# Thirteen waits of GpSimd on VectorE in a fused linear-attention and PReLU feed-forward kernel

## The chip, the cores and the metric

The kernel runs on one core of a Trainium2 chip. The metric is the device time of one execution in microseconds; the median over the runs stands for a kernel. The profile is one further execution, taken by the hardware profiler, whose own time is given beside its span (first to last instruction).

## The reference

Decayed linear attention over blocks, and then a feed-forward layer with a PReLU between its two products (all in float32, cut to what is computed):

```python
# q, k, v: (4, 8, 768, 64); lam: one decay per head; block = 64
for b in range(nb):
    intra = (q_b @ k_b^T * Dmask) @ v_b            # Dmask[i, j] = lam**(i-j) for i >= j, else 0
    inter = (q_b * lam**(pos+1)) @ kv_state
    out_b = intra + inter
    kv_state = lam**block * kv_state + (k_b * lam**(block-1-pos))^T @ v_b
x = out as (3072 tokens, 512)
h = x @ w_in                                       # 512 x 2048
g = maximum(h, 0) + alpha * minimum(h, 0)
y = g @ w_out                                      # 2048 x 512
```

## The kernel before

The tokens are worked through in six groups `c` of 512 (256 positions of two batches). Each group has four attention units, numbered 4c to 4c+3 (a batch and four of the eight heads), so there are 24 units, of which each works on two blocks of 128 positions. The attended output of a group is written, transposed and in float16, to `XT[c]`, and is the moving operand of the first product of the feed-forward layer.

For unit n the steps are: `cast` (queries or keys to float16), `turn` and `turn_copy` (TensorE transpose into PSUM, and its copy to `qkT`; later units use a DMA transpose, `turned`), `decayed` (L336: queries times decay, to `qdT`), `key_decayed` (L281: keys times decay, to `kdec`), `score_products` and `masked` (L385: scores times the decay mask, to `sm`), then on TensorE `inter` (queries with the state `R`), `intra` (`sm` with the values), `state_products` (keys with values), and after these `attended` (L431: PSUM to `XT`), `first_state` (L447: the new state after the first block, on ScalarE) and `states` (L453: the decayed state plus the new product, on VectorE). `inter`, `intra` and `state_products` of all units share one PSUM tile, `acc`, so that `inter` of the next unit stands behind `attended`, `first_state` and `states` of the one before.

The feed-forward layer takes group 0 in the plain way: `up` (16 blocks of 128 hidden features), `relu` on ScalarE and `prelu` (L513) on VectorE, `down` into `o_ps`. From group 1 on the second product, and for groups 4 and 5 the first one too, is made by a scheme of seven products in place of eight (Strassen-Winograd), which needs sums and differences of operand quarters: `w_sum(i, k)` (L558) for `w_out`, `in_sum(i, k)` (L694) for `w_in`, `g_sum` (L580) for the hidden activations, `x_sum` for the inputs. `i` says which sum, `k` which quarter of it. Each of these calls is one subtraction or addition of two float16 operands of 128x512 in SBUF (lines L550 and L553), on VectorE, or on GpSimd where the last argument is `"G"`. The product in seven parts begins at the call `second(1, 1, 0)`, long behind the place of the change.

The program is written out by hand as one list of calls (L776 to L1818). The order of the calls is the order of each engine's own instructions; between engines the framework puts semaphore waits where data or buffers demand them. Nothing else keeps, say, GpSimd behind VectorE. GpSimd also issues DMAs (`load_v16`, `load(..., "G")`, `load_win`, `load_wout`), in the same order as its other instructions; the other loads, the stores and the DMA transposes stand in the queue of SyncE.

The calls that the change touches stand in the list as follows: `w_sum(1, 0)` at L1023 (t1 on VectorE, between `decayed(7, "V")` and `attended(5, "V")`), `key_decayed(6)` at L996 (GpSimd), `in_sum(1, 0)` at L1061, `cast(9, "q16", "G")` at L1040, `decayed(8)` at L1072 and `w_sum(2, 0)` at L1077.

Of the kernel before, what the change touches and what calls it, by code (L numbers as in the profile page):

```python
# [11 lines left out]
def kernel(  # L12
# [229 lines left out]
    XT = {}  # L242
    units = [(c, bi, hh) for c in range(NC) for bi in range(2) for hh in range(2)]

    def copy_on(eng, out, in_):
        if eng == "A":
            nc.scalar.activation(out, in_, AF.Copy)  # L247
        elif eng == "V":
            nc.vector.tensor_copy(out=out, in_=in_)
        else:  # L250
            nc.gpsimd.tensor_copy(out=out, in_=in_)
# [178 lines left out]

    def attended(n, eng):  # L431
        co, bo, ho = units[n]
        if co not in XT:
            pool, tag = (raw_pool, "kraw") if co == 5 else (xt_pool, "xT")
            XT[co] = pool.tile([128, NHP, 2, 2, L], fp16, tag=tag, name="xT")
        copy_on(
            eng,
            XT[co][:, ds(2 * ho, 2), :, bo, :].rearrange("p h e (a j) -> p a (h e) j", a=2),
            acc[:, :, 0:256].rearrange("p a (he j) -> p a he j", j=64),
        )  # L440

# [66 lines left out]
    def relu(c, f, bi=None):  # L508
        n = CH if bi is None else W
        m = M[c, f, bi] = m_pool.tile([128, CH], fp32, tag="m", name="m")  # L510
        nc.scalar.activation(m[:, 0:n], HP[c, f, bi][:, 0:n], AF.Relu, scale=-1.0)  # L511

    def prelu(c, f, bi=None):  # L513
        g, m, h = g_of(c, f), M[c, f, bi], HP[c, f, bi]
        if bi is None:
            g = g.rearrange("p e b j -> p (e b j)")
        else:
            g = g[:, :, bi, :]
            m, h = (y[:, 0:W].rearrange("p (e j) -> p e j", e=2) for y in (m, h))
        nc.vector.scalar_tensor_tensor(  # L520
            out=g, in0=m, scalar=oma[:, f : f + 1], in1=h, op0=ALU.mult, op1=ALU.add
        )
# [23 lines left out]
    T_OUT = {}  # L546
    HALF = DM // 2

    def sub(out, a, b, eng="V"):
# [251 lines left out]
    query_decay(1, 1)  # L801
    cast(0, "q16", "V")
    turn(1, (1,))
    turn_copy(1, (1,), "V")
# [23 lines left out]
    cast(2, "k16", "A")  # L828
    cast(3, "q16", "G")
    turn(2, (0,))  # L830
    turn_copy(2, (0,), "V")
# [59 lines left out]
    up(0, 6)  # L891
    prelu(0, 4, 0)
    relu(0, 5)
# [39 lines left out]
    prelu(0, 1)  # L933
    prelu(0, 4, 1)
    relu(0, 0)
# [59 lines left out]
    turn_copy(6, (0,), "V")  # L995
    key_decayed(6)  # L996
    masked(5)
# [5 lines left out]
    key_decayed(7, "V")  # L1003
    decayed(6, "V")
    turn_copy(7, (1,), "A")
    down(0, 3, 2)
# [12 lines left out]
    load(2, 0, "k", 1)  # L1019
    decayed(7, "V")  # L1020
    down(0, 2, 3)
    down_copy(0, 3)
    w_sum(1, 0)  # L1023
    attended(5, "V")
# [14 lines left out]
    first_state(6)  # L1039
    cast(9, "q16", "G")  # L1040
    down_store(0, 2)
# [13 lines left out]
    state_products(8)  # L1055
    w_sum(3, 0)
    query_decay(3, 0)
    w_sum(4, 3)
    load(3, 1, "k", 1)
    prelu(1, 3, 0)  # L1060
    in_sum(1, 0)  # L1061
    score_products(8)
# [8 lines left out]
    up(1, 0)  # L1071
    decayed(8)  # L1072
    states(6, (1,))
    w_sum(3, 3)
    key_decayed(11)
    key_decayed(9)
    w_sum(2, 0)  # L1077
    masked(8)
# [21 lines left out]
    up(1, 15)  # L1100
    w_sum(3, 1)
    up(1, 5)
    relu(1, 7)
# [35 lines left out]
    decayed(9)  # L1139
    prelu(1, 3, 1)  # L1140
    w_sum(3, 2, "G")
    relu(1, 9)
    load_v16(14)
# [50 lines left out]
    second(1, 6, 0)  # L1194
    g_sum(1, 4, 0, 0)
    masked(10)
    g_sum(1, 4, 1, 1, "G")
# [3 lines left out]
    inter(10)  # L1201
    g_sum(1, 4, 1, 0, "G")
    key_decayed(17, "A")
    intra(10)
# [260 lines left out]
    second(2, 5, 1)  # L1465
    decayed(22, "V")
    cast(23, "k16", "G")
    prelu(3, 9)
# [17 lines left out]
    prelu(3, 7)  # L1486
    g_sum(3, 1, 0, 1, "G")
    relu(3, 14)
    second_store(1, 7)
# [359 lines left out]
```

## Time and profile before

| what | value |
|---|---|
| median of 3 runs | 203.97 us (203.88 to 205.3) |
| the profiled execution's own time | 205.24 us |
| its span, first to last instruction | 203.5 us |
| mean granted TensorE clock | 0.989 |
| busy: TensorE, VectorE, GpSimd, ScalarE | 195.1, 175.3, 143.6, 130.9 us |

A row of the timeline gives start in the span, duration, engine, line of the program, operation, output<-input, shape and, in brackets, how long the engine had been idle before it and what released it. Rows that follow one another with the same name are merged, with their count. The records of neighbouring instructions of one engine overlap by some 0.05 to 0.1 us. Buffer numbers are left out in names, so that `t<-w_out_sb` is `w_sum(1, k)` and `t<-w_out_sb,t` is `w_sum(2, k)` or `w_sum(4, k)`.

### The profile page before, as it was taken

The page shows a single profiled execution, that of the slowest core. Times are in us where ns is not written, and L with a number is a line of the kernel's source. Part 1 is how long each engine was busy: PE and PEld are TensorE (multiplying, and loading weights), DVE is VectorE, ACT ScalarE, POOL GpSimd, SP SyncE. Part 2 cuts the span into 40 slices and gives each one's busy share as a digit, 9 for nine tenths or more (in the row PEclk, how much of TensorE's full clock was granted, in tenths as well). Part 3 has the DMA queues.
Part 4 walks back from the last instruction along what each step waited for, and adds up shares of the span by engine and source line. Part 5 has one row for each costly group of instructions (what it writes and reads, how often), then busy time and mean ns, then how long its engine had stood idle before and what let it go on. Part 6 is the DMA issues. An engine that isn't in the chain of part 4 may idle for free.

```text
span 203.5 us, 5865 instructions
## 1 busy us (share of the span) xinstructions
PE 195.1 (96%) x2351; PEld 129.9 (64%) x2351; DVE 175.3 (86%) x320; ACT 130.9 (64%) x281; POOL 143.6 (71%) x161
## 2 busy tenths in 40 slices
PE   7999999995999999999999999999999999999992
PEld 7775454544544498766565768766665656788892
DVE  6988789998989999899999998889989999995800
ACT  5895774426587699687777769455596987533022
POOL 8999859794495948999999979970386222656700
PEclk9999999998899999999999999999999999999999
DMA  5999999999949998999999953230040001103143
GB/s 163 280 196 228 242 269 231 199 291 224 229 52 180 278 239 236 205 223 168 196 293 169 132 77 80 78 106 0 0 156 3 0 2 52 55 19 138 45 152 116
DMA packets 59199, 30.53 MB, mean 150 GB/s; under 512 B 29652, under 2 KB 57956, under 8 KB 59172
## 3 DMA queue, kind: packets, MB, share of 16 engines
q1 hardware_dynamic: 41236, 19.87, 40.1%
q0 software_dynamic: 17776, 10.23, 35.7%
q8 instruction: 18, 0.29, 0.6%
q14 instruction: 9, 0.07, 0.1%
q10 hardware_dynamic: 160, 0.07, 0.1%
HBM read 27.27 MB, written 6.29 MB: 165 GB/s over the span
## 4 chain that ended last, share of the span: by engine, by line
PE 80%; DVE 6%; DMA 4%; POOL 4%; issue 2%; ACT 1%; DVEq 0%; POOLq 0%; ACTq 0%
PE h_ps L498 26%; PE y L632 16%; PE b L632 12%; PE b L757 5%; DMA w_in_sb<-in_moe_w_in_dram 4%; PE o_ps L528 4%; PE e L757 3%; PE a L757 3%; PE acc L402 3%; PE s L377 3%; PE acc L361 2%; POOL v L272 2%; PE acc L422 1%; DVE sm L388 1%; PE tp L316 1%
## 5 line engine op out<-in xcount | busy, mean ns | idle before, releaser
L498 PE MATMUL h_ps<-xT,w_in_sb 128*128 128x512 f16 (+1 forms) x264 | 59.6, 373 | 0.2 <-DMA w_in_sb<-in_moe_w_in_dram 0.2
L632 PEld LDWEIGHTS <-g 128*128 128x128 f16 x464 | 44.7, 98 | 10.1 <-DVE g L550 0.6
L520 DVE SCALAR_TENSOR_TENSOR g<-m,oma,h_ps 128x512 f16<-128x512 f32 (+1 forms) x66 | 46.0, 727 | 3.9 <-ACT m L511 2.8
L511 ACT ACTIVATE m<-h_ps 128x512 f32<-128x512 f32 (+1 forms) x66 | 37.4, 582 | 15.8 <-PE h_ps L498 14.8
L498 PEld LDWEIGHTS <-w_in_sb 128*128 128x128 f16 x264 | 24.4, 98 | 25.5 <-DMA w_in_sb<-in_moe_w_in_dram 1.1
L388 DVE TENSOR_TENSOR sm<-s,dmask 128x1024 f16<-128x1024 f32 x24 | 29.3, 1219 | 2.2 <-PE s L377 2.2
L632 PE MATMUL y<-w_out_sb,g 128*128 128x256 f16 x224 | 27.9, 273 | 0.3 <-DVE g L550 0.3
L550 POOL TENSOR_TENSOR g<-g 128x512 f16<-128x512 f16 x11 | 13.2, 1204 | 16.4 <-DVE s L553 16.3
L341 POOL TENSOR_TENSOR qdT<-qkT,qdecay 128x512 f16<-128x512 f16 (+1 forms) x20 | 21.0, 1056 | 4.7 <-ACT qkT L247 2.6
L632 PE MATMUL b<-t,g 128*128 128x256 f16 x160 | 19.8, 273 | 0.0
L247 ACT ACTIVATE xT<-acc 128x512 f16<-128x512 f32 x22 | 13.1, 595 | 9.6 <-PE acc L422 5.6
L272 POOL DMA_DIRECT2D v<-in_v_dram x24 | 18.8, 789 | 0.0
L457 DVE SCALAR_TENSOR_TENSOR R<-R,rdecay,acc 128x128 f16<-128x128 f16 x54 | 15.6, 342 | 2.8 <-ACT xT L247 2.2
L550 POOL TENSOR_TENSOR g<-g,g 128x512 f16<-128x512 f16 x12 | 14.3, 1204 | 5.0 <-DVE g L550 2.9
L553 POOL TENSOR_TENSOR s<-g,g 128x512 f16<-128x512 f16 x9 | 10.4, 1155 | 8.4 <-DVE g L520 8.4
L528 PE MATMUL o_ps<-w_out_sb,g 128*128 128x512 f16 x64 | 16.1, 395 | 0.0
L247 ACT ACTIVATE o_sb<-y 128x512 f32<-128x512 f32 (+2 forms) x12 | 6.2, 526 | 13.1 <-PE y L674 7.1
L290 ACT ACTIVATE kdec<-kraw,kdecay 128x64 f16<-128x64 f32 x56 | 14.0, 343 | 0.0
L292 POOL TENSOR_TENSOR kdec<-kraw,kdecay 128x512 f16<-128x512 f32 x13 | 13.8, 1068 | 0.0
L361 PE MATMUL acc<-qdT,R 128*128 128x128 f16 x80 | 8.4, 219 | 2.2 <-DVE R L457 2.0
L377 PE MATMUL s<-qkT 64*64 64x128 f16 x384 | 10.3, 222 | 0.2
L402 PE MATMUL acc<-sm,v 64*64 64x128 f16 x384 | 10.1, 224 | 0.1
(130 smaller groups left out, 371.0 us busy)
## 6 DMA issues: line engine op xcount, KB each, us to landing
out_dram<-o_sb SPq DMA_DIRECT2D x23, 256.0 KB, 2.5
kraw<-in_k_dram SPq DMA_DIRECT2D x7, 512.0 KB, 5.8
qraw<-in_q_dram SPq DMA_DIRECT2D x6, 512.0 KB, 5.6
v<-in_v_dram POOLq DMA_DIRECT2D x24, 128.0 KB, 5.2
w_in_sb<-in_moe_w_in_dram POOLq DMA_DIRECT2D x4, 512.0 KB, 7.9
w_out_sb<-in_moe_w_out_dram POOLq DMA_DIRECT2D x4, 512.0 KB, 9.6
qraw<-in_q_dram POOLq DMA_DIRECT2D x6, 256.0 KB, 7.1
qraw<-in_q_dram SPq DMA_DIRECT2D x6, 256.0 KB, 5.6
```

Source lines behind the costliest of these rows:

```text
L247: nc.scalar.activation(out, in_, AF.Copy)
L272: nc.gpsimd.dma_start(out=v16.rearrange("p h e d -> p h (e d)"), in_=v[2 * (c % 2) + bi, ds(4 * hh, 4), ds((c // 2) * W, W), :].rearrange( ...
L341: engine(eng).tensor_tensor(out=qdT[:, :, :, p], in0=(t["qps"] if eng == "P" else t["qkT"][:, 0])[:, :, :, p], in1=qdecay[:, hh, :, :, p], ...
L377: nc.tensor.matmul(t["s"][ds(a * 64, 64), hl, hp, 1 - e, :].rearrange("p (e j) -> p e j", e=2), lhsT=t["qkT"][p, 1, e, hp, ds(a * 64, 64)] ...
L388: nc.vector.tensor_tensor(out=t["sm"].rearrange("p a h x j -> p (a h) x j"), in0=t["s"].rearrange("p a h x j -> p (a h) x j"), in1=mask_of ...
L498: nc.tensor.matmul(h[:, 0:n] if bi is None else h[:, 0:n].rearrange("p (e j) -> p e j", e=2), lhsT=w_in_sb[:, gi, ts(f, 128)], rhs=x.rearr ...
L511: nc.scalar.activation(m[:, 0:n], HP[c, f, bi][:, 0:n], AF.Relu, scale=-1.0)
L520: nc.vector.scalar_tensor_tensor(out=g, in0=m, scalar=oma[:, f : f + 1], in1=h, op0=ALU.mult, op1=ALU.add)
L528: nc.tensor.matmul(O[c, t], lhsT=g_of(c, f)[:, t // 2, t % 2, :], rhs=w_out_sb[:, f, :], start=(f == 0), stop=(f == NF - 1),)
L550: engine(eng).tensor_tensor(out=out, in0=a, in1=b, op=ALU.subtract)
L632: nc.tensor.matmul(Y[c, k][:, ds(b * HALF, HALF)], lhsT=left(c, i, f, b), rhs=right(i, f), start=(f == 0 and b == 0 and i in (1, 5)), stop ...
L757: nc.tensor.matmul(t, lhsT=w, rhs=x, start=(g == 0 and i in (1, 5)), stop=(g == 1), skip_group_check=True)
```

## The change

A new helper, `vector_turn(n)`, remembers the VectorE instruction that was issued last, and `gpsimd_waits(m)` makes the GpSimd instruction that was issued last wait for the remembered one of number m. There are thirteen calls of the second. They fall on eight GpSimd instructions, since some wait for two or three. Some calls change their place in the list, so that the remembered instruction stands ahead of the one that waits. `attended` and `prelu` are rewritten with options that no call uses; what they issue is the same.

```diff
+    TURN = {}
+    def newest(engine_type):
+        return next(i for i in reversed(tc.nc.cur_bb.bb.instructions) if i.engine == engine_type)
+    def vector_turn(n):
+        TURN[n] = newest(mybir.EngineType.DVE)
+    def gpsimd_waits(n):
+        tc.add_manual_dep(
+            newest(mybir.EngineType.Pool),
+            TURN[n].name,
+            mybir.DependencyInfo(mybir.DependencyClass.Sync, mybir.DependencyReason.DATA),
+            reason="VectorE goes first",
+        )
...
     cast(0, "q16", "V")
+    vector_turn(0)
...
     cast(3, "q16", "G")
+    gpsimd_waits(0)
...
     turn_copy(6, (0,), "V")
-    key_decayed(6)
+    w_sum(1, 0)
+    vector_turn(1)
     masked(5)
...
     key_decayed(7, "V")
     decayed(6, "V")
+    vector_turn(2)
+    decayed(7, "V")
+    vector_turn(3)
+    key_decayed(6)
+    gpsimd_waits(2)
+    gpsimd_waits(1)
+    gpsimd_waits(3)
...
-    decayed(7, "V")
     down(0, 2, 3)
     down_copy(0, 3)
-    w_sum(1, 0)
     attended(5, "V")
...
-    cast(9, "q16", "G")
+    in_sum(1, 0)
+    vector_turn(4)
...
     w_sum(3, 0)
+    vector_turn(5)
+    w_sum(4, 3)
+    vector_turn(6)
+    cast(9, "q16", "G")
+    gpsimd_waits(6)
+    gpsimd_waits(4)
+    gpsimd_waits(5)
     query_decay(3, 0)
-    w_sum(4, 3)
     load(3, 1, "k", 1)
-    prelu(1, 3, 0)
-    in_sum(1, 0)
+    prelu_half(1, 3, 0)
...
-    decayed(8)
     states(6, (1,))
     w_sum(3, 3)
+    vector_turn(7)
+    w_sum(2, 0)
+    vector_turn(8)
+    decayed(8)
+    gpsimd_waits(8)
     key_decayed(11)
+    gpsimd_waits(7)
+    gpsimd_waits(8)
     key_decayed(9)
-    w_sum(2, 0)
...
     w_sum(3, 1)
+    vector_turn(9)
...
     w_sum(3, 2, "G")
+    gpsimd_waits(9)
...
     g_sum(1, 4, 0, 0)
+    vector_turn(10)
...
     g_sum(1, 4, 1, 0, "G")
+    gpsimd_waits(10)
...
     decayed(22, "V")
+    vector_turn(11)
...
     g_sum(3, 1, 0, 1, "G")
+    gpsimd_waits(11)
```

What it does to the engines' instructions is seen in three places. The order is unchanged on TensorE, ScalarE, GpSimd and SyncE; on VectorE two instructions move, and on GpSimd seven get a wait for VectorE that they had not, or a later one.

The first place is on VectorE, where the scores of unit 5 are masked. `sm` is written by `masked(5)`, `t1` by `w_sum(1, 0)`, `t2` and `t4` by `w_sum(2, 1)` and `w_sum(4, 1)`, `kdec` by `key_decayed(7)`, `qdT` by `decayed(6)` and `decayed(7)`, `xT` by `attended(5)`. Before:

```order
L249 COPY qkT_983<-tp_978 128x512 [waits PE_49,Pool_49]
L388 TENSOR_TENSOR sm_987<-s_905,dmask_175 128x1024 [waits DVE_49]
L550 TENSOR_TENSOR t2_963<-w_out_sb_122,t1_818 128x512 [waits DMASW7_49]
L550 TENSOR_TENSOR t4_1001<-w_out_sb_122,t2_963 128x512 [waits DVE_49]
L292 TENSOR_TENSOR kdec_1003<-kraw_709,kdecay_176 128x512 [waits DMASW3_49]
L341 TENSOR_TENSOR qdT_1005<-qkT_983,qdecay_181 128x4x64
L341 TENSOR_TENSOR qdT_1086<-qkT_961,qdecay_181 128x4x64
L550 TENSOR_TENSOR t1_818<-w_out_sb_122 128x512 [waits DMASW1_49]
L249 CAST xT_973<-acc_126 128x2x4x64 [waits PE_49,Activation_49]
```

and with the change (the lines of the same helpers have other numbers there):

```order
L249 COPY qkT_983<-tp_978 128x512 [waits PE_49,Pool_49]
L573 TENSOR_TENSOR t1_818<-w_out_sb_122 128x512 [waits DMASW1_49]
L388 TENSOR_TENSOR sm_986<-s_905,dmask_175 128x1024 [waits DVE_49]
L573 TENSOR_TENSOR t2_963<-w_out_sb_122,t1_818 128x512 [waits DMASW7_49]
L573 TENSOR_TENSOR t4_1000<-w_out_sb_122,t2_963 128x512 [waits DVE_49]
L292 TENSOR_TENSOR kdec_1002<-kraw_709,kdecay_176 128x512 [waits DMASW3_49]
L341 TENSOR_TENSOR qdT_1004<-qkT_983,qdecay_181 128x4x64
L341 TENSOR_TENSOR qdT_1006<-qkT_961,qdecay_181 128x4x64
L249 CAST xT_973<-acc_126 128x2x4x64 [waits PE_49,Activation_49]
```

`w_sum(1, 0)` moved from just ahead of `attended(5)` to just ahead of `masked(5)`; the others kept their order.

The second place is on GpSimd, from `load_v16(8)` (the first row) over `cast(6, "k16")`, `key_decayed(6)`, `key_decayed(8)`, `cast(10, "k16")`, `cast(9, "q16")`, `load_v16(9)` and `cast(10, "q16")` to `decayed(8)`. The difference with its waits:

```order
 L272 DMA v_969<-in_v_dram 128x4x128
 L251 CAST qk_922<-kraw 128x512 [waits DMAHW5_49]
-L292 TENSOR_TENSOR kdec<-kraw,kdecay 128x512
+L292 TENSOR_TENSOR kdec<-kraw,kdecay 128x512 [waits DVE_49]
 L292 TENSOR_TENSOR kdec<-kraw,kdecay 128x512 [waits DMAHW6_49]
 L251 CAST qk_1111<-kraw 128x512 [waits DMAHW0_49,PE_49,Pool_49]
-L251 CAST qk_1152<-qraw 128x512 [waits DMAHW7_49,PE_49,Pool_49]
+L251 CAST qk_1245<-qraw 128x512 [waits DMAHW7_49,DVE_49,PE_49]
 L272 DMA v_1278<-in_v_dram 128x4x128 [waits DMASW4_49]
 L251 CAST qk_1111<-qraw 128x512 [waits DMAHW2_49]
-L341 TENSOR_TENSOR qdT<-qkT,qdecay 128x512 [waits Activation_49]
+L341 TENSOR_TENSOR qdT<-qkT,qdecay 128x512 [waits DVE_49,Activation_49]
```

Three instructions gained a wait for VectorE: `key_decayed(6)` for `decayed(7)`, `cast(9, "q16")` for `w_sum(4, 3)`, `decayed(8)` for `w_sum(2, 0)` (of several remembered instructions the last one counts).

The third place is on VectorE behind `masked(7)`, where `qkT` is written by `turn_copy(6)`, `t1` by `w_sum(1, 2)`, `qk16` by `cast(8, "q16", "V")` and `sm` by `masked(6)`. Before, and then with the change:

```order
L388 TENSOR_TENSOR sm_1108<-s_1062,dmask_175 128x1024 [waits PE_49]
L249 COPY qkT_983<-tp_1101 128x512 [waits PE_49]
L550 TENSOR_TENSOR t1_818<-w_out_sb_122 128x512
L249 CAST qk16_1149<-qraw_1021 128x512 [waits DMAHW7_49]
L388 TENSOR_TENSOR sm_1202<-s_1167,dmask_175 128x1024 [waits PE_49]
```

```order
L388 TENSOR_TENSOR sm_1108<-s_1065,dmask_175 128x1024 [waits PE_49]
L249 COPY qkT_983<-tp_1101 128x512 [waits PE_49]
L576 TENSOR_TENSOR s1_775<-w_in_sb_121 128x512
L573 TENSOR_TENSOR t1_818<-w_out_sb_122 128x512
L249 CAST qk16_1149<-qraw_1024 128x512 [waits DMAHW7_49]
L388 TENSOR_TENSOR sm_1201<-s_1166,dmask_175 128x1024 [waits PE_49]
```

`in_sum(1, 0)`, which writes `s1`, came in ahead of `w_sum(1, 2)`; before, it stood behind `prelu(1, 3, 0)`.

More of the change, by code (lines that the diff above doesn't have):

```diff
@@ L429, in state_products, with attended @@
                         )
-    def attended(n, eng):
+    def attended(n, *how):
         co, bo, ho = units[n]
@@ L435, in attended @@
             XT[co] = pool.tile([128, NHP, 2, 2, L], fp16, tag=tag, name="xT")
[L436 to L440, printed above, removed]
+        x = XT[co][:, ds(2 * ho, 2), :, bo, :].rearrange("p h e (a j) -> p a (h e) j", a=2)
+        o = acc[:, :, 0:256].rearrange("p a (he j) -> p a he j", j=64)
+        if len(how) == 2:
+            x, o = x[:, how[0]], o[:, how[0]]
+        copy_on(how[-1], x, o)
     KV = {}
@@ L511, in relu, with prelu, prelu_half, prelu_of @@
         nc.scalar.activation(m[:, 0:n], HP[c, f, bi][:, 0:n], AF.Relu, scale=-1.0)
-    def prelu(c, f, bi=None):
+    def prelu(c, f, eng="V"):
+        prelu_of(c, f, None, eng)
+    def prelu_half(c, f, bi):
+        prelu_of(c, f, bi, "V")
+    def prelu_of(c, f, bi, eng):
         g, m, h = g_of(c, f), M[c, f, bi], HP[c, f, bi]
@@ L519, in prelu @@
             m, h = (y[:, 0:W].rearrange("p (e j) -> p e j", e=2) for y in (m, h))
-        nc.vector.scalar_tensor_tensor(
+        engine(eng).scalar_tensor_tensor(
             out=g, in0=m, scalar=oma[:, f : f + 1], in1=h, op0=ALU.mult, op1=ALU.add
@@ L891 @@
     up(0, 6)
-    prelu(0, 4, 0)
+    prelu_half(0, 4, 0)
     relu(0, 5)
@@ L933 @@
     prelu(0, 1)
-    prelu(0, 4, 1)
+    prelu_half(0, 4, 1)
     relu(0, 0)
@@ L1139 @@
     decayed(9)
-    prelu(1, 3, 1)
+    prelu_half(1, 3, 1)
     w_sum(3, 2, "G")
+    gpsimd_waits(9)
     relu(1, 9)
```

## Prediction

> **What bounds the kernel now.** I read the page first, then the waits and the windows around the one deep hole in TensorE, then the timelines of VectorE, GpSimd and TensorE there.
>
> ```profile
> span 203.5 us, 5865 instructions
> PE 195.1 (96%) x2351; PEld 129.9 (64%) x2351; DVE 175.3 (86%) x320; ACT 130.9 (64%) x281; POOL 143.6 (71%) x161
> PE   7999999995999999999999999999999999999992
> ```
>
> TensorE is busy for 195.1 of 203.5 us. The row of slices shows a ramp at the start, the drain at the end, and one hole in between, the 5 of slice ten. An edit that doesn't touch the hole has little to win. The waits from 43 to 50 us name it:
>
> ```profile
> ACT R L449 <- DVE xT L249: 3.1, 1, 3.1
> PE acc L361 <- DVE R L457: 2.0, 1, 2.0
> ```
>
> TensorE waits 2.0 us, once, for the state update of unit 7 (`states(7)`, L457), which follows `first_state(7)` on ScalarE (L449), which waits for `attended(5)` on VectorE (L249). The windows show a second cost (columns: stretch, its length, busy PE, PEld, DVE, ACT and POOL, granted clock):
>
> ```profile
> 45.56:48.98 3.42, 1.40 (x18) 0.92 (x18) 2.97 (x5) 1.83 (x4) 1.87 (x4) 1.00 1.20 254
> 48.98:52.39 3.41, 3.38 (x57) 2.01 (x56) 2.92 (x7) 1.30 (x4) 1.29 (x2) 0.50 0.89 196
> 52.39:55.80 3.41, 3.41 (x69) 2.14 (x68) 3.41 (x8) 2.62 (x7) 1.61 (x2) 1.00 0.95 245
> ```
>
> In the stretch with the hole TensorE was busy for 1.40 of 3.42 us (41%); in the next stretch of that length the granted clock was 0.50, and then 1.00 again. So the hole seems to be paid twice. VectorE tells where it comes from:
>
> ```profile
> 39.24 1.22 DVE L388 TENSOR_TENSOR sm<-s,dmask 128x1024 f16<-128x1024 f32 x1
> 40.37 0.87 DVE L550 TENSOR_TENSOR t<-w_out_sb,t 128x512 f16<-128x512 f16 x2
> 41.16 0.68 DVE L292 TENSOR_TENSOR kdec<-kraw,kdecay 128x512 f16<-128x512 f32 x1
> 41.77 1.71 DVE L341 TENSOR_TENSOR qdT<-qkT,qdecay 128x256 f16<-128x256 f16 x2
> 43.40 3.11 DVE L550 TENSOR_TENSOR t<-w_out_sb 128x512 f16<-128x512 f16 x1
> 46.44 0.68 DVE L249 CAST xT<-acc 128x512 f16<-128x512 f32 x1
> 47.56 0.61 DVE L457 SCALAR_TENSOR_TENSOR R<-R,rdecay,acc 128x128 f16<-128x128 f16 x2 [0.45 <-ACT R L449]
> 48.08 1.22 DVE L388 TENSOR_TENSOR sm<-s,dmask 128x1024 f16<-128x1024 f32 x1
> 49.55 0.42 DVE L550 TENSOR_TENSOR t<-w_out_sb 128x512 f16<-128x512 f16 x1
> ```
>
> The same subtraction takes 0.42 us at 49.55 (`w_sum(1, 2)`) and 3.11 us at 43.40 (`w_sum(1, 0)`, just ahead of `attended(5)`). GpSimd, meanwhile:
>
> ```profile
> 38.35 1.17 POOL L553 TENSOR_TENSOR s<-w_in_sb 128x512 f16<-128x512 f16 x1
> 41.18 1.69 POOL L550 TENSOR_TENSOR t<-w_out_sb,t 128x512 f16<-128x512 f16 x1 [1.66 <-DMA w_out_sb<-in_moe_w_out_dram]
> 42.81 0.79 POOL L272 DMA_DIRECT2D v<-in_v_dram  x1
> 43.59 0.62 POOL L251 CAST qk<-kraw 128x512 f16<-128x512 f32 x1
> 44.17 2.05 POOL L292 TENSOR_TENSOR kdec<-kraw,kdecay 128x512 f16<-128x512 f32 x2
> 47.77 0.61 POOL L251 CAST qk<-kraw 128x512 f16<-128x512 f32 x1 [1.55 <-DMA kraw<-in_k_dram]
> 48.32 0.61 POOL L251 CAST qk<-qraw 128x512 f16<-128x512 f32 x1
> ```
>
> The slow subtraction ends at 46.51, 0.29 us after `key_decayed(6)` and `key_decayed(8)` (44.17 to 46.22). I take it that VectorE with two operands in SBUF and GpSimd exclude one another, and that the one that waits ends some 0.3 us after the other is done. `decayed(6)` and `decayed(7)` (1.71 us together) lose time in the same way to `w_sum(2, 3, "G")` at 41.18.
>
> The Trainium skill ("SBUF — State Buffer", section "Who interferes with whom") says that such a pair shares a port as a lock, held for a whole instruction by whichever issues first, while the other blocks fully. The first half agrees with the 0.29 us. The second does not: `w_sum(1, 0)` began at 43.40, ahead of the cast at 43.59, and was passed by three instructions. By the rule alone it would have ended by 43.40 + 0.42 = 43.82, and something other than GpSimd would have held it: that is rival C.
>
> **The change part by part.** *1. `w_sum(1, 0)` moves ahead of `masked(5)`* to 39.24, where `in_sum(1, 3, "G")` runs to 39.52, so that it ends by 39.52 + 0.29 = 39.81. `masked(5)` then runs from 39.73 to 40.95 and `w_sum(2, 1)` to about 41.3. Bounds of this part's stall: 0 and 0.15. Next, `w_sum(2, 3, "G")`, which a DMA releases at 41.18, now comes ahead of `w_sum(4, 1)`. It needs 1.17 us (as its like at 38.35) and is done at about 42.45, `w_sum(4, 1)` at 42.75, `key_decayed(7)` at 43.35. TensorE takes that one's `kdec` in the L422 of this view:
>
> ```profile
> 43.38 0.42 PE L402 MATMUL acc<-sm,v 64*64 64x128 f16 x16
> 43.62 0.29 PE L422 MATMUL acc<-v,kdec 64*64 64x64 f16 x16
> 43.75 0.40 PE L377 MATMUL s<-qkT 64*64 64x128 f16 x16
> 44.08 1.90 PE L528 MATMUL o_ps<-w_out_sb,g 128*128 128x512 f16 x8
> 45.81 0.39 PE L316 MATMUL tp<-ident,qk 128*128 128x128 f16 x4
> 48.22 0.27 PE L361 MATMUL acc<-qdT,R 128*128 128x128 f16 x2 [2.02 <-DVE R L457]
> 49.36 0.64 PE L402 MATMUL acc<-sm,v 64*64 64x128 f16 x16
> 52.36 0.63 PE L316 MATMUL tp<-ident,qk 128*128 128x128 f16 x8
> ```
>
> There, at 43.62, 0.27 us are left. `decayed(6)` and `decayed(7)` need about 0.4 each (at 41.77 the first was held until 42.87 + 0.29 = 43.16, and the pair ended at 43.48); between them stands `cast(6, "k16")` of GpSimd, which costs them 0.6 + 0.3 at most. They end between 44.0 and 44.5.
>
> *2. `key_decayed(6)` waits for `decayed(7)`.* Without that, it and `key_decayed(8)` could pass `decayed(7)` as they passed `w_sum(1, 0)`. It starts at 44.5 in place of 44.17. Behind it on GpSimd stand `key_decayed(8)` (then done at 46.6) and `cast(10, "k16")`, which a DMA releases only at 47.77, so nothing is pushed on.
>
> *3. `attended(5)`* so starts at 44.4 in place of 46.44, 2.0 us earlier, and with it `first_state(7)`, `states(7)` (47.56) and `masked(7)` (48.08). `inter(7)` becomes ready at 46.2, just as TensorE ends its transposes (45.81 + 0.39). **The hole of 2.02 us goes.** Bounds: 1.0 (if two more blockings of 0.5 fall into the chain) and 2.1 (`masked(7)` still sets `intra(7)`, and can't come more than 0.1 earlier than the rest allows).
>
> *4. The half clock* goes with the hole. From `intra(7)` at 49.36 to the transposes at 52.36 lie 3.0 us. At full clock the same pieces, by the starts of the rows from 43.38 on, take 0.24 (L402), 0.33 (L377), 0.86 (four of the eight L528, 45.81 − 44.08 = 1.73 for eight) and some 0.25 for small products: 1.7 us. So 1.3 us are won; bounds 0 and 1.4.
>
> *5. The third place costs a little.* `in_sum(1, 0)` (0.42) now stands ahead of `w_sum(1, 2)` and of `cast(8, "q16", "V")`, which feeds the transposes at 52.36. With `cast(10, "k16")` at 47.77 crossing, that cast ends at about 49.15 and TensorE is ready at 49.05: 0.15 lost; bounds 0 and 0.5.
>
> *6. `cast(9, "q16")` waits for `w_sum(4, 3)`, `decayed(8)` for `w_sum(2, 0)`.* The rows are:
>
> ```profile
> 51.93 0.42 DVE L550 TENSOR_TENSOR w_out_sb<-w_out_sb 128x512 f16<-128x512 f16 x1
> 52.26 0.42 DVE L550 TENSOR_TENSOR t<-w_out_sb,t 128x512 f16<-128x512 f16 x1
> 54.23 1.40 DVE L550 TENSOR_TENSOR t<-w_out_sb,t 128x512 f16<-128x512 f16 x1
> ```
>
> ```profile
> 54.19 1.16 POOL L341 TENSOR_TENSOR qdT<-qkT,qdecay 128x512 f16<-128x512 f16 x1 [2.58 <-ACT qkT L247]
> ```
>
> `w_sum(4, 3)` ended at 52.68. Now it comes behind `cast(8, "q16", "V")` (49.15), `masked(6)` (1.2, as at 48.08) and `w_sum(3, 0)` (0.34), so at 51.0. The cast goes from 48.32 to there, and what is queued behind it on GpSimd goes with it: the `v` DMA (0.79), `cast(10, "q16")` (0.61) and `decayed(8)` (1.16), which ends at about 51.0 + 0.6 + 0.8 + 0.6 + 1.2 = 54.2 in place of 55.35 − 3.2 = 52.15. TensorE asks for it in `inter(8)`, at 59.78 (row below) − 3.2 = 56.6: 2.4 us of cover. If that were gone, each microsecond of lateness would cost one. The stall of `w_sum(2, 0)` (1.40 for 0.42) goes, under the same cover.
>
> ```profile
> 59.78 0.39 PE L361 MATMUL acc<-qdT,R 128*128 128x128 f16 x4
> ```
>
> *7. The other new waits* are met already: `w_sum(3, 2, "G")` starts at 64.63, its VectorE partner ends at 61.71, and the three others too start behind their partner's end, so that they cost nothing; the cover is GpSimd's own work ahead of them, and without it each would cost GpSimd, not TensorE, the wait for one short instruction.
>
> ```profile
> 61.28 0.43 DVE L550 TENSOR_TENSOR w_out_sb<-w_out_sb 128x512 f16<-128x512 f16 x1
> ```
>
> ```profile
> 64.63 1.16 POOL L550 TENSOR_TENSOR w_out_sb<-w_out_sb 128x512 f16<-128x512 f16 x1
> ```
>
> **Sum:** 2.0 + 1.3 − 0.15 = 3.2 (3.15), and behind 56 us TensorE runs without a hole, so the shift should reach the end. The profiled execution took 205.24 us, 1.74 more than its span: 205.24 − 3.2 = **202.0**. The median of 203.97 is 1.27 us lower than that execution, the size of term 4; I read it as executions in which the hole is split so that no half clock follows. They lose terms 3 and 5 alone: 203.97 − 1.85 = 202.1, which agrees.
>
> **The rivals.** *A: the half clock is in the median's executions too,* and the 1.27 us are the profiler's. Then 203.97 − 3.2 = 200.8. For it speaks that profiling may cost time; against it, that one plain run took 205.3.
>
> *B: the clock drop has nothing to do with the hole* and stays. Then only terms 3 and 5 come off the profiled execution: 205.24 − 1.85 = 203.4. The 41% ahead of it speak against this. The Trainium skill ("TensorE: Matmul & The Clock Gate", section "What's actually happening") lets the clock fall after an idle window of about 3.4 us; by that, a gap of 2.02 us would not suffice, and the result would be this rival's. The trace agrees with the window's length, not with the need for a wholly idle one.
>
> *C: the stall travels with the instruction.* If `w_sum(1, 0)` waits for something else than GpSimd, it takes 3.11 us at 39.24 too. The sum of VectorE's work ahead of `attended(5)` is the same, which again starts at 46.44: no change, 204.0. Against it: the end 0.29 us after GpSimd's.
>
> *D, slower: `w_sum(4, 1)` is passed as `w_sum(1, 0)` was.* It stands between `w_sum(2, 3, "G")`, the `v` DMA and `cast(6, "k16")`, which end at 42.45, 43.24 and 43.86. Then `w_sum(4, 1)` ends at 44.15, `key_decayed(7)` at 44.8, and TensorE waits at 43.62 for `kdec`, 1.2 us; `inter(7)` comes at 47.4 in place of 48.22, and if the half clock follows this hole too, 205.24 − 0.8 = 204.4, 0.2% above the median. It decides once `key_decayed(7)` ends after 43.62. For it: that order of three has been passed once. Against: `decayed(6)`, in a like place, was not.
>
> **How the numbers follow.** My forecast 0.60, A 0.13, B 0.07, C 0.12, D 0.08. A measurement of this kernel can tell about 1% from no change, that is 201.93 or less as faster, over 206.0 as slower. Half of the forecast lies under 201.93, since its terms spread by 0.4 us: 0.30, with A 0.43 for faster. Slower by over 1% needs D with more than its price: 0.04. The rest, 0.53, is within 1%. The range 200.7 to 203.8 leaves out a part of A (0.05), most of C (0.10) and a half of D (0.04).
>
> **What would show it.** Right: `w_sum(1, 0)` in some 0.5 us near 39.3; `attended(5)` near 44.4; no idle of TensorE over 0.5 us from 43 to 50; a granted clock of 1.00 from 48.98 on; `decayed(8)` ending 2 us ahead of `inter(8)`. Wrong: a gap of TensorE at its L422 near 43.6 (D), a subtraction of 3 us at 39 (C), a half clock without a hole (B), or new idle of TensorE behind 56 us that gives the shift back.

## The result, and the profile after

| | before | changed |
|---|---|---|
| median, 6 executions each, by turns on the same chip | 204.78 us (203.88 to 205.54) | 201.68 us (201.59 to 201.78) |
| ratio, 95% interval | | 0.985 (0.982 to 0.988) |
| profiled execution, its span | 205.24, 203.5 us | 201.59, 199.8 us |
| mean granted clock of the profiled execution | 0.989 | 0.999 |

The change takes 1.5% off the median (1.1% against the 203.97 us that stood before the prediction). As striking is the spread: 1.7 us over six executions before, 0.2 us after. The page of the changed kernel, in the rows that were read before:

```profile
span 199.8 us, 5865 instructions
PE 193.7 (97%) x2351; PEld 129.1 (65%) x2351; DVE 172.7 (86%) x320; ACT 130.9 (66%) x281; POOL 143.0 (72%) x161
PE   7999999999999999999999999999999999999992
```

The 5 in slice ten is gone. The windows in that place (columns as before):

```profile
45.56:48.98 3.42, 3.29 (x73) 2.25 (x71) 3.42 (x8) 2.59 (x6) 1.16 (x2) 1.00 1.28 279
48.98:52.39 3.41, 3.41 (x68) 2.01 (x66) 3.41 (x9) 2.84 (x8) 2.37 (x5) 1.00 1.04 307
```

TensorE is busy for 3.29 us where it was for 1.40, and the granted clock is 1.00 where it was 0.50. VectorE in the timeline of the changed kernel (L573 is the subtraction or addition that was L550, L576 the one that was L553):

```profile
39.06 0.72 DVE L573 TENSOR_TENSOR t<-w_out_sb 128x512 f16<-128x512 f16 x1
39.71 1.21 DVE L388 TENSOR_TENSOR sm<-s,dmask 128x1024 f16<-128x1024 f32 x1
40.84 1.75 DVE L573 TENSOR_TENSOR t<-w_out_sb,t 128x512 f16<-128x512 f16 x2
42.51 0.68 DVE L292 TENSOR_TENSOR kdec<-kraw,kdecay 128x512 f16<-128x512 f32 x1
43.12 1.16 DVE L341 TENSOR_TENSOR qdT<-qkT,qdecay 128x256 f16<-128x256 f16 x2
44.20 0.68 DVE L249 CAST xT<-acc 128x512 f16<-128x512 f32 x1
45.33 0.60 DVE L457 SCALAR_TENSOR_TENSOR R<-R,rdecay,acc 128x128 f16<-128x128 f16 x2 [0.45 <-ACT R L449]
...
57.65 1.37 DVE L573 TENSOR_TENSOR w_out_sb<-w_out_sb 128x512 f16<-128x512 f16 x1
```

GpSimd in the same stretch:

```profile
38.33 1.16 POOL L576 TENSOR_TENSOR s<-w_in_sb 128x512 f16<-128x512 f16 x1
41.16 1.16 POOL L573 TENSOR_TENSOR t<-w_out_sb,t 128x512 f16<-128x512 f16 x1 [1.66 <-DMA w_out_sb<-in_moe_w_out_dram]
...
44.36 2.05 POOL L292 TENSOR_TENSOR kdec<-kraw,kdecay 128x512 f16<-128x512 f32 x2 [0.37 <-DVE qdT L341]
48.67 0.61 POOL L251 CAST qk<-kraw 128x512 f16<-128x512 f32 x1 [2.26 <-DMA kraw<-in_k_dram]
50.32 0.61 POOL L251 CAST qk<-qraw 128x512 f16<-128x512 f32 x1 [1.04 <-PE o_ps L534]
...
52.24 1.17 POOL L341 TENSOR_TENSOR qdT<-qkT,qdecay 128x512 f16<-128x512 f16 x1
...
57.65 1.08 POOL L292 TENSOR_TENSOR kdec<-kraw,kdecay 128x512 f16<-128x512 f32 x1
58.65 0.84 POOL L251 CAST qk<-kraw 128x512 f16<-128x512 f32 x1
59.46 1.16 POOL L341 TENSOR_TENSOR qdT<-qkT,qdecay 128x512 f16<-128x512 f16 x1
```

And TensorE:

```profile
43.45 0.29 PE L422 MATMUL acc<-v,kdec 64*64 64x64 f16 x16
...
45.64 0.39 PE L316 MATMUL tp<-ident,qk 128*128 128x128 f16 x4
45.98 0.27 PE L361 MATMUL acc<-qdT,R 128*128 128x128 f16 x2
...
48.75 0.61 PE L316 MATMUL tp<-ident,qk 128*128 128x128 f16 x8
...
56.15 0.39 PE L361 MATMUL acc<-qdT,R 128*128 128x128 f16 x4
```

`w_sum(1, 0)` takes 0.72 us at 39.06, `key_decayed(6)` starts when `decayed(7)` releases it, `attended(5)` comes at 44.20, and `inter(7)` follows the transposes at 45.98 without idle time: at 48.22 in the profile before, it stood behind 2.02 us of it. The transposes that began at 52.36 now begin at 48.75, 3.61 us earlier, and the profiled execution as a whole is 3.65 us shorter. No idle stretch of TensorE behind 43 us exceeds 0.33 us.

One row is new, and it decides what follows: at 57.65 `w_sum(3, 1)` meets `key_decayed(15)` of GpSimd and takes 1.37 us, ending 0.29 us after it. In the profile before it took 0.43 at 61.28 and met at most the end of a cast.

The experiments below are told by their executions, not by a ratio: each is made in 6 to 12 executions, and on this one core these fall into groups, the shortest of which lies 1% or more below the others, so that a ratio that leaves out the longer ones would leave out the finding.

### The profile page after: what moved, and what is told of

Read it like the earlier page. It is cut to its first block, busy times and chain, and to the rows that moved or that the text cites. A ratio compares the mean times of both kernels' runs of the same rounds, so it can differ in the third digit from the quotient of the medians.

```text
span 199.8 us, 5865 instructions
## 1 busy us (share of the span) xinstructions
PE 193.7 (97%) x2351; PEld 129.1 (65%) x2351; DVE 172.7 (86%) x320; ACT 130.9 (66%) x281; POOL 143.0 (72%) x161
## 4 chain that ended last, share of the span: by engine, by line
PE 84%; DVE 10%; ACT 3%; issue 1%; ACTq 0%; DVEq 0%
PE h_ps L498 27%; PE y L655 16%; PE b L655 12%; PE b L780 5%; PE o_ps L534 4%; PE acc L402 4%; PE s L377 3%; PE a L780 3%; PE e L780 3%; DVE sm L388 2%; PE acc L361 2%; PE tp L316 2%; DVE dmask L195 1%; PE acc L422 1%; DVE t L573 1%; ACT xT L247 1%
## 5 line engine op out<-in xcount | busy, mean ns | idle before, releaser
L573 POOL TENSOR_TENSOR g<-g 128x512 f16<-128x512 f16 x11 | 13.2, 1204 | 16.3 <-DVE s L576 16.3
L573 POOL TENSOR_TENSOR g<-g,g 128x512 f16<-128x512 f16 x12 | 14.3, 1206 | 5.0 <-DVE g L573 2.9
L576 POOL TENSOR_TENSOR s<-g,g 128x512 f16<-128x512 f16 x9 | 10.4, 1156 | 8.4 <-DVE g L526 8.4
L534 PE MATMUL o_ps<-w_out_sb,g 128*128 128x512 f16 x64 | 15.3, 379 | 0.0
L251 POOL CAST qk<-kraw 128x512 f16<-128x512 f32 x10 | 6.5, 654 | 5.0 <-DMA kraw<-in_k_dram 5.0
```

The costliest lines, as they stand in the source:

```text
L534: nc.tensor.matmul(O[c, t], lhsT=g_of(c, f)[:, t // 2, t % 2, :], rhs=w_out_sb[:, f, :], start=(f == 0), stop=(f == NF - 1),)
L573: engine(eng).tensor_tensor(out=out, in0=a, in1=b, op=ALU.subtract)
```

## The experiments

In the order before, GpSimd's `key_decayed(15)`, `cast(11)`, `decayed(9)` and `w_sum(3, 2, "G")` stand in this order behind one another; with the first hole gone, VectorE reaches `w_sum(3, 1)` just there. I call the meeting at `w_sum(1, 0)` the first place, this one the second, and GpSimd instructions that stand so close behind one another a train. VectorE is let in where it runs between two instructions of a train, and passed where further ones run ahead of it. An execution wins a place where VectorE goes first or is let in early, and loses it where it is passed. All executions, by device time and mean granted clock:

| kernel | executions | 201.5 to 202.8 us | 202.9 to 204.2 us | 204.3 us and more, clock 0.995 and more | clock 0.992 and less |
|---|---|---|---|---|---|
| before (all that ran beside the experiments) | 86 | 16 | 12 | 38 | 20 (205.15 to 206.56) |
| changed | 6 | 6 | 0 | 0 | 0 |
| e1: all moves, no waits | 12 | 5 | 2 | 5 | 0 |
| e2: before + one wait | 12 | 7 | 0 | 5 | 0 |
| e3: first place only | 12 | 2 | 0 | 8 | 2 |
| e4: one move, no wait | 7 | 4 | 0 | 2 | 1 |
| e5: change without first place | 12 | 6 | 1 | 0 | 5 |
| e6: before, hole filled | 6 | 0 | 3 | 3 (one at 204.27) | 0 |
| e7: first place + one wait | 6 | 6 | 0 | 0 | 0 |
| e8: change without waits 4 to 8 | 6 | 5 | 0 | 0 | 1 |
| e9: change without wait 9 | 6 | 2 | 0 | 4 | 0 |
| e10: before + two waits | 12 | 12 | 0 | 0 | 0 |
| e11: change without waits 1 to 3 | 12 | 11 | 1 | 0 | 0 |
| e12: change, wait 9 one later | 12 | 7 | 5 | 0 | 0 |

**e1, all moves and no waits.**

```diff
     def gpsimd_waits(n):
+        return
```

> All moves of the change, none of its thirteen waits. Theory (GpSimd passes a waiting VectorE subtraction or product): key_decayed(6) is free to start at 43.95, behind its cast, while decayed(7) is still waiting for that cast (in the changed kernel it runs until 44.28); if it is passed, decayed(7) ends at 46.2 + 0.3 as w_sum(1, 0) did, the hole of 2.0 us is back and the time is 203.9 to 205.5. If VectorE is let in between the cast and key_decayed(6), the time is that of the change, 201.7. Rival (the moves do it all, the waits are inert): 201.7, and no VectorE instruction over 1.5 us ahead of attended(5).

Measured: 203.57 us median, 201.72 to 205.49. The same program takes 201.9 or 205 us from one execution to the next. So the moves alone reach the full gain in some executions, and the waits make it sure. The profiled one (201.85 us) won both places; what the losing ones lost to is not seen.

**e2, one wait, nothing on VectorE moved.** `key_decayed(6)` goes behind `w_sum(1, 0)` in the list and waits for it.

```diff
-    key_decayed(6)
     masked(5)
...
     decayed(6, "V")
+    decayed(7, "V")
+    w_sum(1, 0)
+    vector_turn(1)
+    key_decayed(6)
+    gpsimd_waits(1)
...
-    decayed(7, "V")
     down(0, 2, 3)
     down_copy(0, 3)
-    w_sum(1, 0)
```

> The kernel before with one wait: key_decayed(6) on GpSimd waits for w_sum(1, 0), which stays in its old place just ahead of attended(5); VectorE's order is that of before. Theory (GpSimd holds w_sum(1, 0) up): w_sum(1, 0) is at most held by the cast ahead (until 44.2 + 0.3), attended(5) starts by 44.5, the hole goes, 201.6 to 202.0. Rival (the stall belongs to the instruction or its data): w_sum(1, 0) still takes 3 us, key_decayed(6) starts after it near 46.5, and the time is 204 to 206.

Measured: 202.12 us median; seven executions at 201.66 to 202.21, five at 204.51 to 205.03. The profiled one, 204.51 us, has no hole at the first place. Its VectorE and its GpSimd show where the time went instead:

```profile
57.80 3.57 DVE L566 TENSOR_TENSOR w_out_sb<-w_out_sb 128x512 f16<-128x512 f16 x1
61.29 2.05 DVE L520 SCALAR_TENSOR_TENSOR g<-m,oma,h_ps 128x512 f16<-128x512 f32 x3
```

```profile
57.23 1.08 POOL L292 TENSOR_TENSOR kdec<-kraw,kdecay 128x512 f16<-128x512 f32 x1
58.22 0.63 POOL L251 CAST qk<-kraw 128x512 f16<-128x512 f32 x1
58.79 1.18 POOL L341 TENSOR_TENSOR qdT<-qkT,qdecay 128x512 f16<-128x512 f16 x1
59.91 1.16 POOL L566 TENSOR_TENSOR w_out_sb<-w_out_sb 128x512 f16<-128x512 f16 x1
61.01 0.80 POOL L272 DMA_DIRECT2D v<-in_v_dram  x1
```

`w_sum(3, 1)` arrives during `key_decayed(15)`, is passed by `cast(11)`, `decayed(9)` and `w_sum(3, 2)`, and ends at 61.37, 0.30 us after the last of them. That is the stall of the first place, at another instruction 14 us later. TensorE pays for it:

```profile
PE h_ps L498 <- DVE g L520: 1.6, 2, 1.2
PE acc L402 <- DVE sm L388: 0.7, 1, 0.7
```

The stall exceeds the instruction's own 0.41 us by 3.16 us, the waits sum to 2.3, so TensorE had some 0.9 us of slack.

**e3, the first place of the change and nothing else.** Its move and one wait (`key_decayed(6)` waits for `decayed(7)`).

```diff
-    key_decayed(6)
+    w_sum(1, 0)
     masked(5)
...
     decayed(6, "V")
+    decayed(7, "V")
+    vector_turn(3)
+    key_decayed(6)
+    gpsimd_waits(3)
...
-    decayed(7, "V")
     down(0, 2, 3)
     down_copy(0, 3)
-    w_sum(1, 0)
```

> The kernel before with the first place of the change alone: w_sum(1, 0) ahead of masked(5), key_decayed(6) waits for decayed(7). Theory: this is the whole gain, 201.7 within 0.2. Rival (the later waits and moves bring part of it): over 202.2.

Measured: 204.64 us median; two executions at 201.9, ten at 204.44 to 206.33. By the prediction's sum, in which the first place holds all of the gain, this kernel would be at 202. In its profile the hole at 46 us is gone too, and the second place is lost:

```profile
57.72 3.58 DVE L566 TENSOR_TENSOR w_out_sb<-w_out_sb 128x512 f16<-128x512 f16 x1
```

**e4, `w_sum(1, 0)` moved, no wait.**

```diff
     key_decayed(6)
+    w_sum(1, 0)
     masked(5)
...
     down_copy(0, 3)
-    w_sum(1, 0)
```

> The kernel before with w_sum(1, 0) ahead of masked(5) and nothing else. Theory: as in the run with all moves and no waits, the outcome hangs on whether key_decayed(6) passes decayed(7): passed, 203.9 to 205.5 with a decayed pair of over 3 us; let in, 201.7. Both runs must fall on the same side. Rival (the move suffices): 201.7 in both.

Measured: four executions at 201.58 to 202.07, three at 205.00 to 205.32. In the profiled one (205.0 us) `decayed(7)` took 0.83 us and was not passed, and `w_sum(3, 1)` took 3.57 us at 58.30. So no wait is needed for the first place to be won in this execution, and the second place is lost again. Neither forecast holds: in e4 as in e1, both outcomes came.

**e6, the hole filled with work.** `score_products(7)` is made five times more (six in all, where the expectation says five), at the place of the hole; it writes the same products again.

```diff
     turn(6, (1,))
+    for _ in range(5):
+        score_products(7, again=True)
```

> The kernel before, with score_products(7) made five times in place of once, at the place where TensorE ran into the 2.02 us hole (each repeat writes the same products to the same tile and takes 0.3 to 0.4 us of TensorE). VectorE, GpSimd and their stall are left as they were. Step 4 of the prediction (a half-busy window brings the half clock): the window behind the hole keeps clock 1.00, the execution takes some 1.3 us less than the kernel before, 203.4 to 203.9 against 204.7, wherever w_sum(1, 0) is stalled. Rival (the clock drop is independent of the hole): clock 0.50 again from about 49 us, time unchanged at 204.7, or longer where the repeats reach past the hole.

Measured: 204.08 to 204.68 us. In the profile `w_sum(1, 0)` takes 3.12 us as ever, TensorE's idle time ahead of `inter(7)` is 0.79 us, and the clock stays:

```profile
45.56:48.98 3.42, 2.63 (x93) 2.01 (x91) 2.97 (x5) 1.70 (x4) 1.89 (x3) 1.00 1.27 271
48.98:52.39 3.41, 3.28 (x69) 2.20 (x69) 3.35 (x8) 1.85 (x5) 1.41 (x3) 1.00 0.90 212
```

That fits step 4, but the kernel before, in the 11 executions beside it, did not show the half clock once either. So the run doesn't separate the two, and the time expected, 203.4 to 203.9, did not come. The profiled execution could not have told them apart either, for where the stretches of 3.41 us begin differs between executions. In the profile before, the clock fell at 48.98 and, behind the last matmuls, at 202.58 us, which is 45 stretches of 3.413 us later. In e6's it fell at the end at 201.26 us; 45 stretches earlier is 47.66 us, and by that estimate a hole of 2 us ahead of 48.36 would have been split over two stretches.

**e7, the first place and one wait at the second:** e3, and `key_decayed(15)` waits for `w_sum(3, 1)`.

```diff
     w_sum(3, 1)
+    vector_turn(9)
...
     key_decayed(15)
+    gpsimd_waits(9)
```

> The kernel before with the first place of the change, and one wait more: key_decayed(15) of GpSimd waits for w_sum(3, 1) of VectorE, which the run of the first place alone showed to take 3.6 us near 57.7 us. New theory (a VectorE subtraction that arrives during a GpSimd instruction is either let in behind it or passed by the whole train, anew in each execution, and the second place of this is w_sum(3, 1)): nearly all executions at 201.5 to 202.1, no gap of TensorE over 0.5 us near 60.8. Rival (the loss behind the first place has another origin than w_sum(3, 1), for example the moves of the third place that are left out here): 204 to 205 in most executions, as the first place alone.

Measured: 201.74 us median, 201.66 to 202.49, six of six. One wait at the second place brings e3 from 204.64 to 201.74. The loss behind the first place is this one meeting.

**e8 and e9, the changed kernel without waits 4 to 8, and without wait 9.**

```diff
     def gpsimd_waits(n):
+        if n in (4, 5, 6, 7, 8):
+            return
```

> The changed kernel with its order, but without the waits of cast(9), decayed(8) and key_decayed(11) (numbers 4 to 8). New theory in its first form (these waits delay GpSimd by about half a microsecond, and so set when w_sum(3, 1) meets key_decayed(15)): a part of the executions, up to most, at 203 to 205, with w_sum(3, 1) at 3.6 us in them. Second form (wait 9 alone, which keeps w_sum(3, 2) of GpSimd behind w_sum(3, 1), bounds the loss): 201.7 in nearly all, or at most 1.2 us more. Step 7 of the prediction (the later waits are inert, the first place does it all): 201.7.

Measured: five executions at 201.60 to 202.09, one at 206.62 with a clock of 0.988. The profile is one of the five; what happened in the sixth is not seen.

```diff
     def gpsimd_waits(n):
+        if n in (9,):
+            return
```

> The changed kernel without its wait number 9 (w_sum(3, 2) of GpSimd no longer waits for w_sum(3, 1)). Step 7 of the prediction (that wait is met already and inert): 201.7. If it is the wait that protects w_sum(3, 1): a part of the executions at 203 to 205, with w_sum(3, 1) at 3.6 us, passed by cast(11), decayed(9) and w_sum(3, 2).

Measured: 205.05 us median; two executions at 201.9, four at 205.0 to 205.24. In the profiled one (205.0 us), VectorE and then GpSimd:

```profile
57.72 4.14 DVE L575 TENSOR_TENSOR w_out_sb<-w_out_sb 128x512 f16<-128x512 f16 x1
```

```profile
57.73 1.08 POOL L292 TENSOR_TENSOR kdec<-kraw,kdecay 128x512 f16<-128x512 f32 x1
58.73 0.63 POOL L251 CAST qk<-kraw 128x512 f16<-128x512 f32 x1
59.30 1.17 POOL L341 TENSOR_TENSOR qdT<-qkT,qdecay 128x512 f16<-128x512 f16 x1
60.42 1.16 POOL L575 TENSOR_TENSOR w_out_sb<-w_out_sb 128x512 f16<-128x512 f16 x1
```

In both profiles the two instructions begin together (57.65 in the changed kernel, 57.72 here). There VectorE was let in behind `key_decayed(15)`, and the cast after it took 0.84 us; here it was passed by four, and the cast took 0.63. Wait 9 is the one of the later waits on which most hangs; waits 0, 10 and 11 were not left out by themselves, and e10 below does without them.

**e5, the change without its first place.** `w_sum(1, 0)`, `decayed(7)` and `key_decayed(6)` stand as before; the rest of the change stays.

```diff
+    key_decayed(6)
-    w_sum(1, 0)
-    vector_turn(1)
     masked(5)
...
-    vector_turn(2)
-    decayed(7, "V")
-    vector_turn(3)
-    key_decayed(6)
-    gpsimd_waits(2)
-    gpsimd_waits(1)
-    gpsimd_waits(3)
...
+    decayed(7, "V")
     down(0, 2, 3)
     down_copy(0, 3)
+    w_sum(1, 0)
```

> The changed kernel without its first place: w_sum(1, 0), decayed(7) and key_decayed(6) stand as before and the three waits of key_decayed(6) are left out; the later moves and waits stay. Theory (two places, each lost or won in each execution): only the first can be lost, so the executions fall into those that win it, about 201.7, and those that lose it, 203.9 to 204.1 at a clock of 0.996 or more and 205.2 to 205.7 at 0.992 or less (the half clock); the executions of before between, 204.4 to 205.1 at full clock, are missing. Median above 203.9. Rival (the later waits do the work and the first place little): 201.7 to 202.2 in most.

Measured: six executions at 201.66 to 201.96, one at 204.07 (clock 0.996), five at 205.40 to 205.96 (0.989 to 0.992), none between. The median, 203.0, came out below the 203.9 that was expected, since half of the executions win the first place by themselves; the groups came as expected. Of the kernel before, 15 of the 29 executions beside it took 204.3 us and more with full clock. With the second place made sure, that group is gone.

**e10, the kernel before with two waits and no VectorE instruction moved:** e2, and wait 9.

```diff
     w_sum(3, 1)
+    vector_turn(9)
...
     w_sum(3, 2, "G")
+    gpsimd_waits(9)
```

> The kernel before with two waits and no VectorE instruction moved: key_decayed(6), moved behind w_sum(1, 0) in the list, waits for it, and w_sum(3, 2) of GpSimd waits for w_sum(3, 1). With the first wait alone, 5 of 12 executions took 204.5 to 205.0. Theory (wait 9 ends the passing of w_sum(3, 1) two instructions earlier, so that its stall is at most some 2.5 us, of which TensorE's slack there, 3.6 us of stall less its 1.2 us gap, takes nearly all): all executions at 201.6 to 202.2, as fast as the changed kernel with its thirteen waits. Rival (waits 4 to 8 or the moves are needed too): some at 204 or more.

Measured: 201.94 us median, 201.63 to 202.77, twelve of twelve; with the first wait alone it was seven of twelve. The profiled execution took 202.58: `w_sum(3, 1)` took 1.71 us, let in behind `key_decayed(15)`, and TensorE then waited 0.7 us for `masked` at 76 us, as it did in e2, e3 and e9, and not in the changed kernel, whose stall was 0.96 us. So a stall of 1.30 us seems to cost something already, and the bound that the expectation gave (2.4 us of slack) was wrong: it took the first of e2's three gaps for all of them.

**e11, the changed kernel without waits 1 to 3.**

```diff
     def gpsimd_waits(n):
+        if n in (1, 2, 3):
+            return
```

> The changed kernel in its order, with key_decayed(6) not waiting for VectorE (waits 1 to 3 left out); waits 4 to 11 stay. Prediction's step 2 (without that wait key_decayed(6) and key_decayed(8) pass decayed(7)): decayed(7) takes some 2.5 us in a part of the executions, and these lose 1 us or more, 203 to 205. Rival (moving w_sum(1, 0) is enough there, the wait only insures): 201.6 to 202.1 in all.

Measured: eleven executions at 201.71 to 201.96, one at 204.20. In the profile `decayed(7)` is let in (0.83 us). Moving `w_sum(1, 0)` is nearly enough at the first place; the waits insure at most against something rare, for what the one execution lost to is not seen.

**e12, wait 9 one instruction later,** on the DMA issue behind `w_sum(3, 2, "G")`.

```diff
     w_sum(3, 2, "G")
-    gpsimd_waits(9)
     relu(1, 9)
     load_v16(14)
+    gpsimd_waits(9)
```

> The changed kernel with its wait number 9 one GpSimd instruction later, on the DMA issue of load_v16(14), so that w_sum(3, 2) of GpSimd itself may again pass w_sum(3, 1). Theory X (a wait for VectorE that stands in GpSimd's queue close behind the train is what lets VectorE in, wherever exactly it stands): 201.6 to 202.1 in all executions, w_sum(3, 1) at 1.4 us or less. Theory Y (the wait works only by holding back w_sum(3, 2), so that a train of three is too short to lose more): as without it, 205 in about two thirds of the executions, w_sum(3, 1) at 3.6 to 4.1 us, ended by the DMA issue that now waits for it.

Measured: seven executions at 201.70 to 202.01, five at 203.90 to 204.17. Neither theory holds: some executions lose, against the first, and they lose 2.2 us and not 3.3, against the second. The profiled execution is one of the seven, in which `w_sum(3, 1)` came 0.8 us ahead of `key_decayed(15)` and took 0.65 us; what the five lost to, and at which place, is not seen.

## Why the prediction was right in the time and wrong in one step

*Step 1, right.* `w_sum(1, 0)` ends at 39.78 (39.81 was predicted), `w_sum(4, 1)` at 42.59 (42.75), `key_decayed(7)` at 43.19 (43.35), and TensorE's L422 starts at 43.45 with 0.26 us to spare (0.27). The pair `decayed(6)`, `decayed(7)` ends at 44.28, in the range of 44.0 to 44.5. That the stall is GpSimd's is shown by e2 and e10, where the subtraction stays in its place and GpSimd alone is held back: none of their 24 executions lies at 202.9 to 204.2 us or has the half clock, where 32 of 86 of the kernel before and 6 of 12 of e5 do. The 0.83 us that it takes in e2's profile would not show it alone, since it takes as little in e5's, without the wait. Rival C falls with this and with the 0.72 us at 39.06, rival D with the 0.26 us at L422.

*Step 2, right in effect.* `key_decayed(6)` starts at 44.36 (44.5), and nothing behind it is pushed on. As an insurance it is worth little: without it, one of twelve executions lost time (e11), and at which place is not seen.

*Step 3, right.* `attended(5)` came at 44.20 (44.4), `inter(7)` 2.24 us earlier, of which 0.18 had been gained ahead of 43 us already.

*Step 4, right in size for the profiled execution.* From `inter(7)` to the transposes it is 2.77 us and was 4.14: 1.37 us, predicted 1.3. Rival B falls, for what these runs can tell: of all executions listed above, none under 205.1 us had a clock of 0.992 or less, and in e5, where only the first place can be lost, five of the six that lost had it and none of the six that won. One lost at full clock (204.07), so the hole does not always bring the half clock. That the stretches lie differently in each execution, as e6 shows, fits the prediction's reading of a hole that is split; no run tests it.

*Step 5, mis-sized.* 0.15 us were charged; nothing was lost. `cast(10, "k16")`, taken to cross at 47.77, was released by its DMA only at 48.67, behind `cast(8, "q16", "V")` (47.98 to 48.40).

*Step 6, right.* `decayed(8)` ended at 53.41 (54.2) and `inter(8)` asked for it at 56.15 (56.6): 2.7 us of cover, predicted 2.4.

*The sum* came out 0.5 us too small, 3.65 against 3.15: 0.24 in step 3, 0.07 in step 4, 0.15 in step 5. That is why the larger chance was given to "within 1%", and the result lay just beyond it.

*Step 7 failed, and with it the sentence behind the sum* that the shift should reach the end since TensorE runs without a hole behind 56 us. It called the other new waits "met already" and so took them to do nothing. In the profile of the changed kernel wait 9 is indeed met when its instruction starts, 1.56 us after `w_sum(3, 1)` has ended (59.02):

```profile
60.58 1.15 POOL L573 TENSOR_TENSOR w_out_sb<-w_out_sb 128x512 f16<-128x512 f16 x1
```

Yet without it time is lost (e9). In the profile before, GpSimd was at this point:

```profile
59.79 1.08 POOL L292 TENSOR_TENSOR kdec<-kraw,kdecay 128x512 f16<-128x512 f32 x1
60.78 0.63 POOL L251 CAST qk<-kraw 128x512 f16<-128x512 f32 x1
63.50 1.17 POOL L341 TENSOR_TENSOR qdT<-qkT,qdecay 128x512 f16<-128x512 f16 x1 [2.09 <-ACT m L511]
```

`w_sum(3, 1)` came at 61.28 there, and found at most the end of a cast, with 2.09 us of idle GpSimd behind it. The shift is not the same for both: with the first place won, VectorE arrives 3.6 us earlier (57.72 in e3), `key_decayed(15)` some 2.6 us (57.16). So VectorE falls into a train that has closed up behind it. The prediction weighed each wait where it stood, and not where its partners would stand after the shift; with the first place alone the time is 204.64 us (e3), not 202. Without wait 9, in e1 to e4 and e9, 24 of 49 executions took 204.3 us and more at full clock; with it in its place (the changed kernel, e5, e8, e10, e11), none of 48, though one of them (e8, 206.62 us at half clock) is not explained. Two pairs differ by wait 9 alone: e2 lost so in five of 12 and e10 in none of 12, e9 in four of six and the changed kernel in none of six. The time predicted was right because the change holds the wait that the prediction called inert; in this part that was luck.

*The reading of the median* was half right. That executions differ by whether the half clock follows is true (20 of 86 have it), and rival A falls, since executions at 203.9 to 204.1 us have a clock of 0.997 and more. But the commonest execution of before is another one, 204.3 us and more at full clock (38 of 86, of which 35 lie at 204.39 to 205.28), which goes away when the second place is made sure (e5). By that, and by the profiles of e2 and e3 (204.51 and 204.45 us), it wins the first place and loses the second; no execution of the kernel before in this group was profiled. And 16 of 86 executions of the kernel before already take 201.5 to 202.1 us, as the changed one does. The change makes no execution shorter than the best of before; it makes that one the rule.

No version ran faster than the changed kernel. e7 (201.74) and e10 (201.94) come near it with two waits, and with idle time of TensorE at 0.33 us or less nothing is left to win in these places.

## What to carry to other kernels

Where one profile shows a stall between two engines that depends on who comes first, look for the next place where the same two would meet once the stall is gone, by moving each engine's rows by its own shift. Look at the list of single times, not only at the median: groups with nothing between them are places won or lost from one execution to the next, and a wait that costs nothing can be worth a per cent because it takes the draw away. Leave out each of several waits in turn: here two waits do nearly all that thirteen do.

## What the runs showed of the hardware

A waiting VectorE subtraction can be passed by several GpSimd instructions that stand close behind one another: three at 57.80 in e2 (3.57 us), four at 57.72 in e9 (4.14 us), with its end 0.3 us after the last one each time. The Trainium skill ("SBUF — State Buffer", section "Who interferes with whom") describes the shared port as a lock held for one instruction by whichever issues first; these rows agree with the exclusion, but it is not first come, first served. In e10 `w_sum(3, 1)` began 0.35 us ahead of `key_decayed(15)` and still ended 0.29 us after it.

At the second place, whether VectorE is let in does not follow from the time of arrival as the trace shows it. It came 565 ns after `key_decayed(15)` had started in e1's profile and was let in (0.82 us); 559 to 571 ns after in those of e2, e3 and e4, and was passed. Three profiles have the two within 10 ns of each other, and three outcomes: VectorE went first in e11 (0.42 us), was let in behind `key_decayed(15)` in the changed kernel (1.37), and was passed by four in e9 (4.14), the one of the three without wait 9. At the first place, with the subtraction and GpSimd in their old order, five profiles go by arrival: where it came 0.19 or 0.20 us ahead of `cast(6, "k16")` (before, e6) it was passed, where it came 0.18 to 0.20 us behind its start (e2, e5, e10) it was let in; five are too few for a rule. Where it was let in behind `key_decayed(15)`, the cast that followed took 0.84 or 0.85 us in place of 0.63 (the changed kernel, e1, e8, e10).

A wait seems to act ahead of the instruction that has it: with wait 9 on `w_sum(3, 2, "G")`, none of 48 executions took 204.3 us or more at full clock, although `cast(11)` and `decayed(9)` stand ahead of it and carry no wait. Not all of these executions meet a train: in e5's profile `w_sum(3, 1)` came 0.78 us ahead of `key_decayed(15)`. By what mechanism the wait lets VectorE in so early was not found; e12 shows only that one place further along it works less well.

A stretch that is half idle does not always bring the half clock. In e9's profile the clock fell at the end at 202.67 us; counted back from there by 42 stretches of 3.413 us, as in e6, one of them begins at 59.31. In it TensorE was busy for 1.61 of 3.42 us (47%), and the clock stayed at 1.00 in the next one:

```profile
59.31:62.73 3.42, 1.61 (x53) 0.99 (x52) 3.42 (x3) 0.64 (x2) 3.40 (x5) 1.00 1.39 206
62.73:66.14 3.41, 3.06 (x16) 1.46 (x15) 3.41 (x5) 2.88 (x6) 2.88 (x4) 1.00 1.17 309
```

The Trainium skill ("TensorE: Matmul & The Clock Gate", section "What's actually happening") ties the drop to an idle window of about 3.4 us. The profile before has the drop behind a stretch that was 41% busy, so a wholly idle one was not needed there. If the busy share decides, the limit lies between 41% and 47% by these two stretches; that it does, no run here shows.
